# Attending the first batch in two halves of its queries, with MoE work beside the second half, and V loaded by a casting transfer

## The chip, the cores and the metric

The kernel runs on one core of one Trainium2 chip. The metric is device microseconds (us) of one execution, as a median over runs. Engines: PE is the matmul engine (PEld its weight loads), DVE the vector engine, ACT the scalar engine, POOL (Pool) GpSimd, SP the engine that issues most transfers. Ratios below are the mean time of one kernel's fast runs over that of the kernel before in the same rounds on the same chip, so they are not quite the ratio of the medians that stand beside them. The brackets behind a ratio are its 95% interval.

## The reference

```python
# q, k, v: [8 batches, 12 heads, 448, 64]; w_in: [768, 2048]; w_out: [2048, 768]
q_n, k_n = rmsnorm(q, g_q), rmsnorm(k, g_k)          # over the last axis
scores = q_n @ k_n.T / 8 ; scores -= max(scores)      # per query
attn = exp(scores) / sum(exp(scores))
x = (attn @ v), heads side by side                    # [3584, 768]
h = x @ w_in ; out = maximum(0.01 * h, h) @ w_out     # float32
```

The last line is called MoE in the kernel. It is two dense matrix products.

## The kernel before

The attention is cut into 24 units: a batch times three groups of four heads. Each unit is prepared (squares on ACT, their sums on DVE, the reciprocal root `rinv` on ACT, the normalised `n` on DVE), transposed to `qkT`, and then attended (scores `sT` on PE, exps `et` on ACT, the product with V on PE). The exps take a bound `eb` in place of the maximum: probe matmuls on PE, maxima `pm` and a diagonal `dg` on DVE, a matmul `pb` on PE, and `cm` and `eb` on DVE. Units 0 and 1 are transposed on PE (`prep_tr`), all later ones by a transpose transfer (`prep_trd`).

```python
def prep_v(u):                      # V arrives as float32, Pool casts it
    nc.gpsimd.tensor_copy(buf(u, "vt")..., hj(raw[u][2])...)
def prep_trd(u):                    # one transfer transposes q and k of a unit
    nc.sync.dma_start_transpose(out=buf(u, "qkT")..., in_=buf(u, "n16")...)
def qk_exp(u, i0, n):               # 8 score blocks and 8 exps a unit, 2 per quarter d
    ...
def moe1(b, ft):                    # 6 matmuls of 448 columns, then the leaky relu on ACT
    ...
for u in range(NU):
    for d in range(NJ):             # NJ = 4 quarters
        qk_exp(u, 2 * d, 2)
        ...                         # cut: unit 0 has its own order
        if d == 0:
            load(u + 3); pv(u - 1); prep_v(u + 2); prep_qg(u + 2, ...); prep_sq(u + 2)
            if u < 5: load_w_out(4 * (u - 1), 4)
        if d == 1 and u % NQ == 0:
            push_moe(u // NQ - 1)   # MoE of a batch, queued when its three units are done
        if d == 2: prep_probe(u + 1); prep_rinv(u + 2); prep_norm(u + 2, ...); prep_trd(u + 2)
        if d == 3: prep_shift(u + 1)
        fill(u, d)                  # takes MoE pieces from the queue
```

In these traces an instruction that waits holds the work that stands behind it on its engine.

Of the kernel before, what the change touches and what calls it, by code (L numbers as in the profile page):

```python
# [8 lines left out]
FP32 = mybir.dt.float32  # L9
FP16 = mybir.dt.float16  # L10
AF = mybir.ActivationFunctionType
# [7 lines left out]
def kernel(  # L19
# [24 lines left out]
    cst = ctx.enter_context(tc.tile_pool(name="cst", bufs=1))  # L44
    raws = ctx.enter_context(tc.tile_pool(name="raws", bufs=2))
    prep_p = ctx.enter_context(tc.tile_pool(name="prep", bufs=2))
# [41 lines left out]
    def load(u, parts=1):  # L88
        b, g = divmod(u, NQ)
        tiles = []  # L90
        for name in ("rq", "rk", "rv"):
            tiles.append(raws.tile([SP, QH, NJ, D], FP32, tag=name, name=name))
        n = QH // parts
        todo = [(i, p) for p in range(parts) for i in range(2)] + [(2, p) for p in range(parts)]
        for i, p in todo:
            src = (q, k, v)[i][b, QH * g + n * p:QH * g + n * p + n]
            nc.sync.dma_start(tiles[i][:, n * p:n * p + n], src.rearrange("h (p j) d -> p h j d", j=NJ))
        raw[u] = tiles
        st[u] = {}

    HJ = QH * NJ
# [3 lines left out]
    def hj(t):  # L105
        return t.rearrange("p h j d -> p (h j) d")

    SHAPES = dict(
        sq=([SP, 2, HJ, D], FP32, 1), ssq=([SP, 2, HJ], FP32, 2), uu=([SP, 2, HJ], FP32, 2),
        rinv=([SP, 2, HJ], FP32, 2), qg=([SP, HJ, D], FP32, 2), vt=([SP, QH, NJ, 2, D // 2], FP16, 4),  # L110
        n16=([SP, 2, 2, NJ, 2, D], FP16, 2), qkT=([128, 2, 2, NJ, SP], FP16, 3))
# [11 lines left out]
    def prep_qg(u, eng, c=ALL):  # L123
        n = c[1] - c[0]
        eng.tensor_tensor(buf(u, "qg")[:, c[0]:c[1]], hj(raw[u][0])[:, c[0]:c[1]],  # L125
                          ggb[:, None, :].broadcast_to([SP, n, D]), op=ALU.mult)

    def prep_v(u):
        nc.gpsimd.tensor_copy(buf(u, "vt").rearrange("p h j t d -> p (h j) t d"),  # L129
                              hj(raw[u][2]).rearrange("p j (d t) -> p j t d", t=2))  # L130

# [18 lines left out]

    def prep_tr(u, r):
        tp = aux([128, 2, NJ, SP], FP16, "tp")
        for ti in range(2):
            for j in range(NJ):
                nc.tensor.transpose(tp[:, ti, j, :],  # L155
                                    buf(u, "n16")[:, ti, r, j].rearrange("p a d -> p (a d)"),
                                    ident16[:SP, :])
        nc.vector.tensor_copy(buf(u, "qkT")[:, :, r], tp)

# [39 lines left out]
    def qk_exp(u, i0, n):  # L199
        s = st[u]  # L200
        if i0 == 0:
            s["et"] = epool.tile([SP, NJ, QH, S], FP16, tag="et", name="et")
        sTs = []
        for i in range(i0, i0 + n):
            r, jk = divmod(i, NJ)
            sT = psum.tile([SP, 2, 512], FP32, tag="sT", bufs=2, name="sT")
            for a in range(2):
                qT, kT = pair_qk(u, r, a)
                nc.tensor.matmul(sT[:, a, 0:S], kT[:, ts(jk, SP)], qT,  # L209
                                 start=True, stop=True)  # L210
            sTs.append(sT)
        for i, sT in zip(range(i0, i0 + n), sTs):
            r, jk = divmod(i, NJ)
            nc.scalar.activation(s["et"][:, jk, 2 * r:2 * r + 2, :], sT[:, :, 0:S], AF.Exp,  # L214
                                 bias=s["eb", r], scale=1.0)

    xts = {}

    def pv(u):
        s = st[u]  # L220
        b, g = divmod(u, NQ)
        if g == 0:
            xts[b] = xpool.tile([128, NQ, 2, S], FP16, tag="xt", name="xt")
        xt = xts[b]
        banks = []
        for w in (2, 0, 1):
            bank = aux([128, 512], FP32, "pv")
            for jk in range(NJ):
                for i in range(QH):
                    lhsT = ones16 if w == 2 else s["vt"][:, i, jk, w, :]  # L230
                    nc.tensor.matmul(bank[32 * i:32 * i + 32, 0:S], lhsT, s["et"][:, jk, i, :],  # L231
                                     start=(jk == 0), stop=(jk == NJ - 1))
            banks.append(bank)
            if w == 2:
                lz = zpool.tile([128, S], FP32, tag="lz", name="lz")
                nc.scalar.activation(lz, bank[:, 0:S], AF.Ln)
                rz = zpool.tile([128, S], FP32, tag="rz", name="rz")
                nc.scalar.activation(rz, lz, AF.Exp, bias=0.0, scale=-1.0)  # L238
            else:
                nc.vector.tensor_tensor(xt[:, g, w, :], bank[:, 0:S], rz, op=ALU.mult)  # L240

    def moe1(b, ft):
        xt = xts[b]
        hps = aux([128, 512], FP32, "hps")
        for kt in range(KT):
            nc.tensor.matmul(hps[:, 0:S], win16[:, kt // 2, kt % 2, ts(ft, 128)],  # L246
                             xt[:, kt // 2, kt % 2], start=(kt == 0), stop=(kt == KT - 1))
        nc.scalar.activation(gt[:, ft, ds(S * (b % 2), S)], hps[:, 0:S], AF.Prelu,  # L248
                             bias=0.0, scale=1.0, alpha=0.01)
# [25 lines left out]

    def push_moe(b):
        for ft in range(FT):
            queue.append((1.13, lambda b=b, ft=ft: moe1(b, ft)))
        for t in (range(3) if b % 2 == 0 else range(3, 7)):
            for half in range(2):  # L280
                queue.append((2.62, lambda b=b, t=t, half=half: moe2(b // 2, t, half)))
# [4 lines left out]
    def fill(u, d):  # L286
# [3 lines left out]
        while True:  # L290
# [5 lines left out]
            left += WD[dd]  # L296
        debt[0] += total * WD[d] / left
        while queue and debt[0] >= queue[0][0] * 0.5:
# [4 lines left out]
    with tc.manual_schedule():  # L303
        nc.scalar.dma_start(grow[:, 0], g_q[None, :])
        nc.scalar.dma_start(grow[:, 1], g_k[None, :])
        load(0, parts=2)
        load(1)
        nc.scalar.preload_act_table_set("natural_log_exp_and_others")
        nc.vector.tensor_tensor(grow[:, 0], grow[:, 0], grow[:, 1], op=ALU.mult)
# [5 lines left out]
        prep_qg(0, nc.vector, HALF[0])  # L315
        prep_ssq(0, HALF[0])
        prep_rinv(0, HALF[0])
        prep_norm(0, 0)
        prep_tr(0, 0)
        prep_sq(0, HALF[1])  # L320
        prep_probe(0, (0,))
        prep_v(0)
        prep_shift(0, (0,))
        prep_qg(0, nc.vector, HALF[1])
        prep_ssq(0, HALF[1])

        for u in range(NU):
            for d in range(NJ):
                qk_exp(u, 2 * d, 2)
                if u == 0:  # L330
                    if d == 0:
                        prep_rinv(0, HALF[1])
                        prep_norm(0, 1)
                        prep_tr(0, 1)
                        prep_probe(0, (1,))
                        prep_sq(1)
                        prep_v(1)
                        prep_qg(1, nc.vector)
                        prep_ssq(1)
                        load(2)  # L340
                        load_w_in(0, 512)
                        load_w_in(512, 512)
                        load_w_in(1024, 1024)
                        load(3)
                    if d == 1:
                        prep_shift(0, (1,))
                        prep_rinv(1)
                        prep_norm(1, 0)
                        prep_tr(1, 0)
                        prep_norm(1, 1)  # L350
                        prep_tr(1, 1)
                    if d == 2:
                        prep_probe(1)
                        prep_sq(2)
                        prep_v(2)
                        prep_qg(2, nc.vector)
                        prep_ssq(2)
                    if d == 3:
                        prep_shift(1)
                        prep_rinv(2)  # L360
                        prep_norm(2, 0)
                        prep_norm(2, 1)
                        prep_trd(2)
                    continue
                if d == 0:
                    if u + 3 < NU:
                        load(u + 3)
                    pv(u - 1)
                    if u + 2 < NU:
                        prep_v(u + 2)  # L370
                        prep_qg(u + 2, nc.vector if u == 1 else nc.gpsimd)
                        prep_sq(u + 2)
                    if u < 5:
                        load_w_out(4 * (u - 1), 4)
                if d == 1 and u % NQ == 0:
                    push_moe(u // NQ - 1)
                if u + 1 < NU:
# [13 lines left out]
        pv(NU - 1)  # L391
        push_moe(B - 1)
        while queue:
# [31 lines left out]
```

## Time and profile before

| kernel before | value |
|---|---|
| time, median of 4 runs | 471.83 us (471.44 to 472.27) |
| span of the profiled run | 470.1 us |
| first MoE matmul | 66.84 us |
| PE busy | 433.3 us, 92% of the span |
| ACT busy | 322.2 us, 69% |

The prediction below shows the overview, the stretches, the chain of waits and the timeline. Exps on ACT per stretch: stretch, its length, ACT time in exps (their number), granted clock, DMA share, GB/s.

```profile
20.00:40.00 20.00, 6.57 (x8) 1.00 1.14 242
40.00:60.00 20.00, 12.38 (x14) 0.66 1.16 243
60.00:80.00 20.00, 9.43 (x11) 0.83 0.96 175
```

The second view has the chain of waits (start, length, what) within 37 to 45 us, that is while the one transpose transfer of the chain, of unit 2, was under way:

```profile
37.64 7.11 DMA qkT<-n
```

### The profile page before, as it was taken

What the parts mean: (1) busy time and instruction counts of PE and PEld (TensorE: products, weight loads), DVE (VectorE), ACT (ScalarE), POOL (GpSimd) and SP (SyncE); (2) the same over time, 40 slices, a digit from 0 to 9 for tenths busy, and PEclk for the clock granted to TensorE, in tenths of its full rate; (3) what the DMA queues carried; (4) which work ended last, traced back from release to release, by engine and by line L of the source; (5) the groups of instructions that cost most, each with busy time, mean ns of one, the idle gap of its engine ahead of it and who ended that gap; (6) DMA issues with size and microseconds to landing.
All of it is one profiled execution on the core that took longest, in us unless ns stands there. A gap on an engine that the chain in (4) does not pass through costs nothing.

```text
span 470.1 us, 8104 instructions
## 1 busy us (share of the span) xinstructions
PE 433.3 (92%) x3355; PEld 218.6 (47%) x3355; DVE 273.4 (58%) x416; ACT 322.2 (69%) x469; POOL 88.0 (19%) x63
## 2 busy tenths in 40 slices
PE   2255799999999999999999999999999999999995
PEld 1122334455445544455455544454455544555563
DVE  4877656767756957666666766685665761211021
ACT  3558888976896588777877589867877588644400
POOL 1611333212312303320320210220320200000000
PEclk9998669999999999999999999999999999999999
DMA  8899998784485494376457466359438412021022
GB/s 208 172 240 235 250 224 136 169 191 89 135 158 120 107 225 93 72 184 144 112 126 173 95 182 143 66 140 210 79 95 193 106 35 40 0 68 35 0 68 67
DMA packets 82665, 60.95 MB, mean 130 GB/s; under 512 B 42436, under 2 KB 78276, under 8 KB 82628
## 3 DMA queue, kind: packets, MB, share of 16 engines
q1 hardware_dynamic: 78064, 54.14, 49.8%
q0 software_dynamic: 4560, 6.29, 7.9%
q8 instruction: 26, 0.43, 0.4%
q14 instruction: 11, 0.09, 0.1%
q10 hardware_dynamic: 4, 0.00, 0.0%
HBM read 45.61 MB, written 11.01 MB: 120 GB/s over the span
## 4 chain that ended last, share of the span: by engine, by line
PE 80%; DVE 9%; ACT 8%; DMA 2%; issue 1%; ACTq 0%; DVEq 0%
PE op L259 30%; PE hps L246 27%; PE pv L231 11%; PE sT L209 9%; DVE n L145 5%; ACT et L214 5%; DMA qkT<-n 2%; ACT sq L121 1%; PE probe L178 1%; DVE pm L181 1%; PE pb L191 1%; DVE dg L185 1%; PE tp L155 1%; DVE ssq L134 1%; ACT gt L248 1%
## 5 line engine op out<-in xcount | busy, mean ns | idle before, releaser
L214 ACT ACTIVATE et<-sT,eb 112x896 f16<-112x896 f32 x192 | 182.4, 1005 | 82.6 <-PE sT L209 67.9
L246 PE MATMUL hps<-xt,win 128*128 128x448 f16 x768 | 153.2, 353 | 0.0
L259 PE MATMUL op<-wout,gt 128*128 128x384 f16 x896 | 152.7, 326 | 0.0
L259 PEld LDWEIGHTS <-gt 128*128 128x128 f16 x896 | 85.5, 98 | 61.4 <-issue 7.5
L246 PEld LDWEIGHTS <-win 128*128 128x128 f16 x768 | 72.1, 98 | 72.0 <-issue 10.2
L248 ACT ACTIVATE gt<-hps 128x448 f16<-128x448 f32 x128 | 66.4, 542 | 27.5 <-PE hps L246 27.3
L129 POOL CAST vt<-rv 112x1024 f16<-112x1024 f32 x24 | 27.5, 1144 | 279.3 <-DMA rv<-in_v_dram 244.1
L209 PE MATMUL sT<-qkT 64*112 64x448 f16 x384 | 62.2, 395 | 7.8 <-ACT et L214 7.8
L262 DVE COPY ost<-op 128x384 f32<-128x384 f32 x56 | 31.0, 554 | 64.8 <-PE op L259 64.7
L240 DVE TENSOR_TENSOR xt<-pv,rz 128x448 f16<-128x448 f32 x48 | 27.9, 620 | 69.1 <-ACT rz L238 67.5
L145 DVE TENSOR_TENSOR n<-qg,rinv 112x512 f16<-112x512 f32 x48 | 56.3, 1173 | 8.3 <-ACT rinv L140 8.1
L134 DVE TENSOR_REDUCE ssq<-sq 112x16 f32<-112x1024 f32 (+1 forms) x50 | 56.3, 1167 | 0.0
L125 POOL TENSOR_TENSOR qg<-rq,ggb 112x1024 f32<-112x1024 f32 x20 | 51.2, 2559 | 0.0
L145 DVE TENSOR_TENSOR n<-rk,rinv 112x512 f16<-112x512 f32 x48 | 50.8, 1058 | 0.0
L181 DVE TENSOR_REDUCE pm<-probe 112x1 f32<-112x448 f32 (+1 forms) x50 | 28.0, 601 | 38.1 <-PE probe L178 37.3
L231 PE MATMUL pv<-et,vt 112*32 112x448 f16 x768 | 45.1, 381 | 0.0
L209 PEld LDWEIGHTS <-qkT 64*112 64x112 f16 x384 | 20.0, 131 | 44.9 <-issue 44.6
L231 PEld LDWEIGHTS <-vt 112*32 112x32 f16 x768 | 22.1, 104 | 18.8 <-issue 5.3
L121 ACT ACTIVATE sq<-rq 112x1024 f32<-112x1024 f32 (+1 forms) x25 | 25.2, 1007 | 1.0 <-DMA rq<-in_q_dram 1.0
L121 ACT ACTIVATE sq<-rk 112x1024 f32<-112x1024 f32 (+1 forms) x25 | 25.2, 1008 | 0.1
L231 PE MATMUL pv<-et,ones 112*32 112x448 f16 x384 | 24.8, 382 | 0.2 <-DVE cm L193 0.2
L155 PE MATMUL tp<-ident,n 112*128 112x112 f16 x32 | 4.4, 293 | 13.1 <-DVE n L145 12.9
(34 smaller groups left out, 126.5 us busy)
## 6 DMA issues: line engine op xcount, KB each, us to landing
rq<-in_q_dram SPq DMA_DIRECT2D x23, 448.0 KB, 5.6
rk<-in_k_dram SPq DMA_DIRECT2D x23, 448.0 KB, 6.6
rv<-in_v_dram SPq DMA_DIRECT2D x23, 448.0 KB, 7.3
wout<-in_moe_w_out_dram POOLq DMA_DIRECT2D x4, 768.0 KB, 9.5
out_dram<-ost SPq DMA_DIRECT2D x8, 336.0 KB, 2.8
out_dram<-ost SPq DMA_DIRECT2D x8, 288.0 KB, 3.5
out_dram<-ost SPq DMA_DIRECT2D x8, 240.0 KB, 4.6
win<-in_moe_w_in_dram POOLq DMA_DIRECT2D x6, 256.0 KB, 9.3
```

Of the source, the lines that this page charges most:

```text
L121: nc.scalar.activation(buf(u, "sq")[:, ti, c[0]:c[1]], hj(raw[u][ti])[:, c[0]:c[1]], AF.Square)
L125: eng.tensor_tensor(buf(u, "qg")[:, c[0]:c[1]], hj(raw[u][0])[:, c[0]:c[1]], ggb[:, None, :].broadcast_to([SP, n, D]), op=ALU.mult)
L134: nc.vector.tensor_reduce(buf(u, "ssq")[:, ti, c[0]:c[1]], buf(u, "sq")[:, ti, c[0]:c[1]], axis=AXL.X, op=ALU.add)
L145: nc.vector.tensor_tensor(buf(u, "n16")[:, ti, r].rearrange("p j a d -> p a j d"), src[:, 8 * r:8 * r + 8].rearrange("p (a j) d -> p a j d ...
L181: nc.vector.tensor_reduce(pm2[:, a:a + 1], probes[a][:, 0:224 * len(rs)], axis=AXL.X, op=ALU.max)
L209: nc.tensor.matmul(sT[:, a, 0:S], kT[:, ts(jk, SP)], qT, start=True, stop=True)
L214: nc.scalar.activation(s["et"][:, jk, 2 * r:2 * r + 2, :], sT[:, :, 0:S], AF.Exp, bias=s["eb", r], scale=1.0)
L231: nc.tensor.matmul(bank[32 * i:32 * i + 32, 0:S], lhsT, s["et"][:, jk, i, :], start=(jk == 0), stop=(jk == NJ - 1))
L246: nc.tensor.matmul(hps[:, 0:S], win16[:, kt // 2, kt % 2, ts(ft, 128)], xt[:, kt // 2, kt % 2], start=(kt == 0), stop=(kt == KT - 1))
L248: nc.scalar.activation(gt[:, ft, ds(S * (b % 2), S)], hps[:, 0:S], AF.Prelu, bias=0.0, scale=1.0, alpha=0.01)
L259: nc.tensor.matmul(op2[:, 0:HC], gt[:, ft, ts(t, 128)], wout16[:, ft, ds(HC * half, HC)], start=(ft == 0), stop=(ft == FT - 1))
L262: nc.vector.tensor_copy(ost[0][:, ds(HC * half, HC)], op2[:, 0:HC])
```

## The change

Its intent: PE waits in the first 67 us. If the three units of batch 0 are attended for the first half of their queries first, the first half of the batch's tokens has its x early, and the MoE of those tokens can fill PE beside the second half of the queries. Besides, V comes by a transfer that casts it on the way, which takes 24 casts from Pool. To make the start fit, unit 0 is prepared whole, the multiplies `qg` of the first units go from DVE to Pool, and unit 1 now goes through a transpose transfer. The core of the diff:

```diff
-        for name in ("rq", "rk", "rv"):
+        tiles = [... for name in ("rq", "rk")]
+    def load_v(u):
+        nc.gpsimd.dma_start(buf(u, "vt"), v[...])          # casts float32 to float16
-    def prep_v(u): ...
+    SH = S // 2
+    def qk_exp_half(u, half, r): ...                       # 4 exps of a unit's half, 224 queries
-    def pv(u):
+    def pv(u, half=None): ...                              # V weights now two elements apart
-    def moe1(b, ft):
+    def moe1(b, ft, c0, n): ...                            # n = 224 or 448 columns
+        early(0, 0)                # exps of unit 0, half 0; prepares unit 1 (prep_trd) and 2
+        prep_probe(1); prep_shift(1); load(3)
+        early(1, 0); pv(0, 0); early(0, 1); pv(1, 0)
+        prep_probe(2); prep_shift(2); load(4)
+        early(2, 0); ...; pv(0, 1); load_w_out(0, 4); early(1, 1)
+        ...; prep_trd(3); pv(2, 0); load(5); early(2, 1)
+        push_moe1(0, 0, SH)        # MoE, first half of the tokens
+        ...; pv(1, 1); load_w_out(4, 4)
+        spend(4.5)                 # some 4.5 us of MoE from the queue here
+        prep_rinv(4); prep_norm(4, 0); prep_norm(4, 1); prep_trd(4)
+        prep_probe(3); prep_shift(3)
+        spend(4.0)
-        for u in range(NU):
+        for u in range(NQ, NU):    # units from 3 on as before
...                                # cuts: start-up of unit 0, buffer counts
```

## The prediction

> **What bounds the kernel now.** I read the overview of the page first, then stretches of the span, then the chain that ended last, then the timeline of the first 100 us.
>
> The 40 slices (11.75 us each) show two regimes:
>
> ```profile
> PE   2255799999999999999999999999999999999995
> ...
> ACT  3558888976896588777877589867877588644400
> ```
>
> TensorE (PE) is nearly saturated from the seventh slice to the end; before that no engine is. The stretches give the same in microseconds (length, then busy time of PE, PEld, DVE, ACT, POOL, then clock, DMA share, GB/s):
>
> ```profile
> 0.00:67.00 67.00, 35.63 (x257) 15.71 (x258) 45.37 (x85) 43.36 (x60) 21.09 (x26) 0.85 1.05 217
> 67.00:120.00 53.00, 52.83 (x419) 26.45 (x419) 36.07 (x50) 42.14 (x62) 12.25 (x7) 1.00 0.76 162
> 120.00:200.00 80.00, 80.00 (x635) 40.05 (x639) 54.63 (x75) 62.28 (x94) 19.45 (x10) 1.00 0.55 127
> 200.00:300.00 100.00, 99.83 (x794) 50.61 (x787) 68.14 (x94) 77.76 (x115) 21.12 (x12) 1.00 0.59 138
> ```
>
> Busy time alone proves little for PE, but the chain of waits agrees: from the first MoE matmul (66.84) to the last copy it is matmul after matmul.
>
> ```profile
> 66.84 3.52 PE hps L246 x18
> ...
> 426.01 18.31 PE hps L246 x96
> 444.32 20.81 PE op L259 x128
> 465.15 0.56 DVE ost L262
> ```
>
> So: a start of 66.8 us, bound by a chain through ACT, DVE, PE and transfers; then 398.4 us (465.2 - 66.8) of dense PE work; then 5 us of last copy and store, span 470.1. The runs read about 1.7 us more than the span. Only two things can shorten the time: PE getting dense earlier, or less PE work. The change adds no PE speed, so the whole question is when PE gets dense and how much MoE work it has done by then.
>
> How the start hangs together shows in these lines of the timeline (start, length, instruction, idle time and releaser):
>
> ```profile
> 34.90 1.69 PE L231 MATMUL pv<-et,ones 112*32 112x448 f16 x16
> ...
> 45.45 1.16 DVE L181 TENSOR_REDUCE pm<-probe 112x1 f32<-112x448 f32 x2 [1.81 <-PE probe L178]
> ...
> 49.95 1.91 ACT L214 ACTIVATE et<-sT,eb 112x896 f16<-112x896 f32 x2 [2.21 <-DVE eb L195]
> ...
> 73.78 2.79 POOL L125 TENSOR_TENSOR qg<-rq,ggb 112x1024 f32<-112x1024 f32 x1
> ...
> 74.29 2.84 DVE L145 TENSOR_TENSOR n<-rk,rinv 112x512 f16<-112x512 f32 x1
> ...
> 77.99 0.94 PE L231 MATMUL pv<-et,ones 112*32 112x448 f16 x16
> ```
>
> Three readings. The same 16 matmuls take 1.69 us in the start and 0.94 us later. An exp waits for the bound eb, which comes 2.5 us after the probe matmuls even when DVE is free (two maxima 1.16, a small maximum, the diagonal 0.25, a matmul, a maximum, eb). And a normalisation takes 2.84 us beside a Pool multiply instead of its usual 0.68 us.
>
> **What the Trainium skill says.** "TensorE: Matmul & The Clock Gate", Part 1, says that the array runs at half clock until about 3.4 us of sustained work and falls back after an idle window as long. The 1.69 against 0.94 us agrees, though the clock row still reads full there at 35 us. "GPSIMD Engine Reference", 1. Specifications, says that GpSimd shares its SBUF interfaces with VectorE, with contention for DVE instructions with two SBUF inputs; the 2.84 us agree: the multiply ends at 76.57 and the normalisation 0.56 us later. "DMA: Bandwidth & Descriptors", SWDGE vs HWDGE vs iDMA, says a casting transfer must be issued from GpSimd; the weights already come that way (0.71 us of Pool each), so V by such a transfer costs Pool 0.7 us in place of a cast of 1.14 us.
>
> **The V part.** It removes 24 casts of 1.14 us (27 us of Pool) and 24 transfers from the SP queue, and adds 24 casting transfers. In the dense regime neither Pool nor DVE nor DMA (share 0.55 to 0.6) sets the end, so that is worth about 0. The weights of the PV matmuls become columns two elements apart; no trace here has such a load. The 48 matmuls of a unit take 2.38 us, one per 49.6 ns, near what 448 columns in four column groups need, and loads hide under that; I assume they still do. At the very start V of unit 0 now competes with q and k of unit 0, which the first squares wait for (before, V stood behind them in the queue): about 1 us lost.
>
> **The start, walked along the order of the built program** with durations from the trace (squares 1.0 each, four normalisations 2.4, two sums 2.3, exp pair 1.9, transpose transfer 5 to 7, the eb chain 2.5).
> - Unit 0 is prepared whole before any exp. Squares of its second half stand ahead of rinv of the first on ACT, and the sums of unit 1 (2.3 us) ahead of the maxima on DVE. First exp about 22.5 us; in the kernel before 12.3, but there only four exps were done by 21.
> - Four exps and the squares of unit 2 to 28.5. Unit 1 now goes through a transpose transfer; its normalisation stands behind a Pool multiply; the maxima of unit 1 also stand behind the normalisation of unit 2, at 33. Second batch of exps (unit 1) about 36, ACT idle some 6 us before it.
> - Eight exps (with a short PE wait) to 46; then bound of unit 2 after its PV and probe: about 50. Twelve more exps with three reciprocals (2 ACTIVATEs each, estimated 0.4 us at half width), squares of units 3 and 4, rinv: ACT is full to 68. The PV half of unit 1 ends on PE about 67, and there the first half of MoE begins.
>
> So MoE begins at about 67, just where it began before (66.8). All that the halves gained up to here is that PV of unit 2's second half (1.2 us) is not done yet: no gain.
>
> **From there**: 15 of the 16 half-width groups of the first MoE product stand before unit 3. Six matmuls of 195 ns (3.51/18) make 1.17 us at full width, so 0.6 warm and 1.2 cold at half width. Eight groups, some cold: 67 to 73.6. Then PE has probe and bound of unit 3 in its queue, ahead of the other seven. The bound needs the maxima on DVE; those stand behind the normalisation of unit 4; that waits for rinv of unit 4, which stands on ACT behind the eight Prelus. Sum: last Prelu 0.5, ln and exp 0.6, four normalisations 2.4, maxima 1.3, diagonal 0.3 = 5.1 us in which PE can do only the probe. PE resumes at about 79, cold again by its idle time; seven groups 4.2 to 6 us: 85. Scores of unit 3, the last PV half, the sixteenth group and waits for exps: 3 us. **MoE's second half starts at about 88**, where the kernel before stood at 66.8.
>
> Remaining work then: 398.4, less the 16 half groups already done (9.3), plus about 1 for matmuls of 224 columns that cannot run at twice the rate (estimate), plus 1 where units 3 and 4 have so little MoE left that ACT sets the pace (in one quarter of unit 4: 1.9 exps + 1.1 + 2.1 + Prelus against PE's 4.3) = 391. End of span 88 + 391 + 5 = 484, timed 486. I take 2 off because the array may stay warm through part of this: **484.0 us**, 2.6% slower.
>
> **The rivals.**
> 1. The intended gain: the halves pipeline, the start is shorter, and 9.3 us of MoE vanish into idle PE time. By the sum above, the second MoE half would have to begin before 470 - 391 - 5 = 74 merely to break even, and by 65 to be 2% faster. For: ACT has only 48 us of work before that point (43 before, plus 5 of Prelus). Against: the orders above leave ACT idle for some 14 us before the first exp, 6 before unit 1 and 3.5 before unit 2, and nothing in the order fills that. If the first exps come 5 us earlier and the wait at unit 3 is 3 us: 474.
> 2. The array clock falls less often than I assume and Pool's multiplies do not collide with normalisations: 478 to 480, counted as "same".
> 3. It is worse: the strided weight load no longer hides, or half-width matmuls are bound by the 98 ns weight load and more; 0.03 us on 192 matmuls is 6 us; or transposes queue behind 6.3 MB of weights read in the first 42 us: 490 or more.
>
> **Range and chances.** The late wait (5 us), the two ramps of the clock and the missing gain at 67 carry the sum; each start step is good to 1 or 2 us, together 5. Range 475 to 491. The 2% limit is 481.1, a little below the centre: slower 0.66; same 0.29; faster needs 462.2, which the ACT order forbids unless I misread it: 0.05.
>
> **What would show it.** Right: first exp near 22 us; ACT idle before exps of unit 1 and of unit 2; first half-width MoE matmul near 67; a PE gap of 4 to 5 us before the bound of unit 3 that ends on DVE's diagonal; second MoE half near 88; the stretches from 120 on with PE at 100% as before, and the last 40 us the same. Wrong: MoE beginning by 58, or no gap at the bound of unit 3, would mean a start shorter than walked. PV of a full unit over 2.5 us, or half-width matmuls over 115 ns apart, would mean that rival 3 pays. PE gaps after 150 us would mean that the bound moved to ACT or to V's arrival, which I do not expect.

## More of the kernel before

```profile
q0 software_dynamic: 269, 0.50, 33.3%
```

The software queue carries the casting loads of the weights. Their packets took a third of the DMA engines' time while the transpose of unit 2 ran. (The shares of the queues overlap and can add up to more than 100%.)

## The result and the profile after

| | before | after |
|---|---|---|
| time, median | 471.83 us (471.44 to 472.27, 4 runs) | 495.16 us (494.76 to 496.04, 4 runs) |
| ratio | | 1.050 [1.048, 1.052] |
| span | 470.1 us | 493.2 us |
| PE busy | 433.3 us | 435.5 us |
| first MoE matmul | 66.84 us | 73.71 us, half width |

The change costs 23.3 us. PE is busy for only 2.2 us more, so 21 of the 23 us are PE idling. The overview of the kernel after (40 slices, now of 12.3 us each, the digit is the busy share in tenths) has it in the first seven slices:

```profile
PE   1305676999999999999999999999999999999995
ACT  3533693798599676887787758976896578753400
```

Where the kernel before had PE at 5 and 5 in slices three and four and at 7, 9, 9 in five to seven, this one has 0, 5 and 6, 7, 6, and ACT has holes too. The stretches (length, busy time of PE, PEld, DVE, ACT, POOL, then clock, DMA share, GB/s) say when PE becomes dense:

```profile
80.00:93.50 13.50, 9.26 (x105) 7.29 (x105) 4.50 (x10) 4.95 (x12) 3.21 (x4) 0.75 0.92 178
93.50:120.00 26.50, 24.22 (x240) 15.89 (x242) 16.26 (x30) 23.97 (x44) 5.44 (x5) 1.00 0.62 112
120.00:140.00 20.00, 18.69 (x175) 9.70 (x164) 11.21 (x21) 13.88 (x19) 3.05 (x2) 1.00 0.71 168
140.00:200.00 60.00, 59.39 (x460) 30.17 (x460) 32.03 (x57) 45.84 (x69) 12.20 (x8) 1.00 0.60 120
200.00:300.00 100.00, 100.00 (x809) 50.43 (x807) 52.40 (x94) 76.27 (x110) 18.31 (x12) 1.00 0.56 122
```

From 140 us on PE is nearly as full as before (59.39 of 60 us, then 100 of 100), so the loss lies ahead of it. Between 93.5 and 120 us ACT is busy for 23.97 of 26.5 us: there PE loses 2.3 us with ACT nearly full. The timeline of the start (start, length, engine, line, instruction, in brackets the idle time before it and what ended it) shows the rest:

```profile
22.97 3.70 ACT L233 ACTIVATE et<-sT,eb 112x896 f16<-112x896 f32 x4 [1.92 <-PE sT L228]
...
40.38 0.62 PE L178 MATMUL probe<-qkT 64*112 64x224 f16 x4 [14.83 <-DMA qkT<-n]
43.57 3.70 ACT L233 ACTIVATE et<-sT,eb 112x896 f16<-112x896 f32 x4 [12.65 <-PE sT L228]
...
73.71 5.38 PE L265 MATMUL hps<-xt,win 128*128 128x224 f16 x48
...
84.24 0.34 PE L191 MATMUL pb<-dg,onesp 112*112 112x112 f16 x1 [4.82 <-DVE dg L185]
84.38 6.24 PE L265 MATMUL hps<-xt,win 128*128 128x224 f16 x42
...
93.53 2.95 PE L265 MATMUL hps<-xt,win 128*128 128x224 f16 x24
```

After four exps from 22.97 us on, ACT gets no exp until 43.57 us. PE stood 14.83 us at the probe of unit 1, for its transpose. The chain of waits gives that transfer its length:

```profile
28.07 12.26 DMA qkT<-n
```

Of the 23 transpose transfers of this kernel the median took 4.0 us, so this one took three times as long. The DMA queues within 28 to 41 us, the time of this transfer, show what it shared the engines with:

```profile
q0 software_dynamic: 1317, 1.82, 78.6%
```

The casting loads take 78.6% here, against 33.3% beside the transpose of the kernel before, and V is among them now. Last, the exps per stretch, as above:

```profile
20.00:40.00 20.00, 3.70 (x4) 1.00 1.18 192
40.00:60.00 20.00, 10.24 (x12) 0.95 1.05 200
60.00:80.00 20.00, 8.24 (x9) 0.63 0.31 71
80.00:100.00 20.00, 5.47 (x6) 0.83 0.85 155
```

There are 16 exps done by 60 us (26 before) and 25 by 80 us (37 before). The attention is 12 exps behind, which is one and a half units, when the MoE of the first half begins to pay.

### The profile page after: what moved, and what is told of

Read it like the earlier page. It is cut to its first block, busy times and chain, and to the rows that moved or that the text cites. A ratio compares the mean times of both kernels' runs of the same rounds, so it can differ in the third digit from the quotient of the medians.

```text
span 493.2 us, 8643 instructions
## 1 busy us (share of the span) xinstructions
PE 435.5 (88%) x3626; PEld 235.5 (48%) x3626; DVE 224.0 (45%) x408; ACT 326.8 (66%) x493; POOL 82.4 (17%) x67
## 4 chain that ended last, share of the span: by engine, by line
PE 80%; ACT 9%; DVE 5%; DMA 4%; issue 1%; SPq 0%; DVEq 0%; ACTq 0%
PE op L278 30%; PE hps L265 28%; PE pv L251 11%; PE sT L209 8%; ACT et L213 3%; DVE n L145 3%; DMA qkT<-n 2%; ACT et L233 2%; ACT sq L125 2%; DMA rk<-in_k_dram 2%; PE pb L191 1%; PE probe L178 1%; DVE pm L181 1%; PE sT L228 1%; DVE ssq L134 0%
## 5 line engine op out<-in xcount | busy, mean ns | idle before, releaser
L265 PE MATMUL hps<-xt,win 128*128 128x448 f16 (+1 forms) x864 | 157.1, 337 | 0.5 <-DVE cm L193 0.3
L129 POOL TENSOR_TENSOR qg<-rq,ggb 112x1024 f32<-112x1024 f32 (+1 forms) x24 | 55.6, 2315 | 301.8 <-DMA rq<-in_q_dram 276.6
L267 ACT ACTIVATE gt<-hps 128x448 f16<-128x448 f32 (+1 forms) x144 | 68.6, 503 | 36.7 <-PE hps L265 36.5
L259 DVE TENSOR_TENSOR xt<-pv,rz 128x448 f16<-128x448 f32 (+1 forms) x54 | 28.6, 568 | 95.1 <-ACT rz L257 94.7
L209 PE MATMUL sT<-qkT 64*112 64x448 f16 x336 | 50.0, 371 | 3.7 <-ACT et L213 3.6
L251 PE MATMUL pv<-et,vt 112*32 112x448 f16 (+1 forms) x864 | 44.9, 357 | 0.0
L181 DVE TENSOR_REDUCE pm<-probe 112x1 f32<-112x448 f32 x48 | 27.7, 619 | 37.6 <-PE probe L178 36.5
L145 DVE TENSOR_TENSOR n<-qg,rinv 112x512 f16<-112x512 f32 x48 | 33.2, 691 | 23.5 <-ACT rinv L140 14.4
L145 DVE TENSOR_TENSOR n<-rk,rinv 112x512 f16<-112x512 f32 x48 | 35.6, 742 | 0.0
L251 PE MATMUL pv<-et,ones 112*32 112x448 f16 (+1 forms) x432 | 25.0, 358 | 0.0
```

The lines of the kernel that those rows point to most:

```text
L129: eng.tensor_tensor(buf(u, "qg")[:, c[0]:c[1]], hj(raw[u][0])[:, c[0]:c[1]], ggb[:, None, :].broadcast_to([SP, n, D]), op=ALU.mult)
L145: nc.vector.tensor_tensor(buf(u, "n16")[:, ti, r].rearrange("p j a d -> p a j d"), src[:, 8 * r:8 * r + 8].rearrange("p (a j) d -> p a j d ...
L181: nc.vector.tensor_reduce(pm2[:, a:a + 1], probes[a][:, 0:224 * len(rs)], axis=AXL.X, op=ALU.max)
L209: nc.tensor.matmul(sT[:, a, 0:S], kT[:, ts(jk, SP)], qT, start=True, stop=True)
L251: nc.tensor.matmul(bank[32 * i:32 * i + 32, 0:n], lhsT, et[:, jk, i, 0:n], start=(jk == 0), stop=(jk == NJ - 1))
L265: nc.tensor.matmul(hps[:, 0:n], win16[:, kt // 2, kt % 2, ts(ft, 128)], xt[:, kt // 2, kt % 2, ds(c0, n)], start=(kt == 0), stop=(kt == KT ...
```

## The experiments

Two theories stood against each other. **Collisions**: the halves are sound, and the loss is the slow transposes and the wait at the bound of unit 3. **Halves**: the halves lose by themselves, since unit 3 begins only when the second halves are done, and the collisions come on top. All runs gave correct results. A third question was whether V had a part.

### V alone

The kernel before, with V by the casting transfer and the weights of PV two elements apart, and nothing else.

```diff
-        nc.gpsimd.tensor_copy(buf(u, "vt")..., hj(raw[u][2])...)
+        nc.gpsimd.dma_start(buf(u, "vt"), v[b, QH * g:QH * g + QH].rearrange("h (p j) d -> p h j d", j=NJ))
-        lhsT = ... s["vt"][:, i, jk, w, :]
+        lhsT = ... s["vt"][:, i, jk].rearrange("p (d t) -> p t d", t=2)[:, w]
```

> The kernel before with one part of the change alone: V by casting transfers, where the casts stood, and the PV weights at every second column. Theory (V part is worth about nothing, the loss is all in the new order of the start): within 1.5 us of 471.9, PV of a full unit still 2.4 us, TensorE dense from 120 us on. Rival (V by such transfers, or the strided weight loads, cost the time): 476 or more, PV over 2.5 us.

Measured: 473.48 us (472.75 to 474.21, 6 runs) against 471.87, ratio 1.003 [1.001, 1.005]. V is worth 1.6 us of the 23.3 and the strided weights nothing that shows.

### Unit 1 transposed on PE

```diff
-                    prep_trd(1)
+                if (u, half, r) == (0, 0, 1):
+                    prep_tr(1, 0, nc.vector.tensor_copy)
+                    prep_tr(1, 1, nc.vector.tensor_copy)
```

> The changed kernel with one thing undone: unit 1 is transposed by 16 matmuls and two DVE copies, as before the change, instead of by a transfer. Theory (the 12.3 us transpose transfer of unit 1 holds the second batch of exps back): exps of unit 1 begin at about 36 instead of 43.6 us, everything behind them moves by the same 7 us, timed about 488. Rival (the transfer is hidden, because the transfer of unit 2, which landed at 41.9, or another chain would end just as late): under 2 us gained, 493 or more.

Measured: 488.30 us (486.76 to 488.96) against 471.93, ratio 1.034 [1.031, 1.037]. The exps of unit 1 begin at 37.5 us and the second MoE half at 87.4 us. The transfer was worth 6.9 us (495.16 - 488.30).

### The weight loads moved instead

The same wait can be taken away from the other side: the transfer stays, and `w_in` is loaded later.

```diff
-        load_w_in(0, 512); load_w_in(512, 512); load_w_in(1024, 1024)
         prep_rinv(1)
 ...
         prep_qg(3, nc.gpsimd)
+        load_w_in(0, 512); load_w_in(512, 512); load_w_in(1024, 1024)
```

> The changed kernel with the nine loads of the first weights issued behind the Pool multiply of unit 3 (about 47 us) instead of at 16 to 24 us. Theory (the transpose transfer is slow because these loads hold the DMA engines): the transposes of units 1 and 2 land 5 to 6 us after issue, exps of unit 1 begin at about 36 us, and the time falls by about 7 to 488, less what the first MoE matmul then waits for its weights (they need some 20 us, so until 67 to 70, where MoE would begin: 0 to 3 us lost). Rival (a transpose transfer at this place is slow by itself, two in a row): landing still 8 us and more, no gain.

Measured: 492.10 us (491.83 to 493.25), ratio 1.043 [1.040, 1.046]. It is short of the expectation (488, and 0 to 3 us more), and tells the most about the mechanism. The transposes of units 1 and 2 landed in some 4 us now, and the exps of unit 1 began at 35.2 us. But the chain of waits of this run shows that the wait went with the loads:

```profile
62.07 15.24 DMA qkT<-n
77.35 0.66 PE probe L178 x4
```

The transpose of unit 3 was issued beside the moved loads and took 15.2 us, with PE at the probe behind it. To be exact, the last `w_in` load landed at some 63.5 us; what lay beside the rest of this transpose were two `w_out` loads that had been pushed back behind `w_in` (the second landed 21.8 us after its issue, against 9.0 in the kernel after). Casting packets took 74.1% of the engines' time from 62 to 77 us.

### The bound of unit 3 first

```diff
         spend(4.5)
-        prep_rinv(4); prep_norm(4, 0); prep_norm(4, 1); prep_trd(4)
         prep_probe(3)
-        prep_shift(3)
         spend(4.0)
+        prep_shift(3)
+        prep_rinv(4); prep_norm(4, 0); prep_norm(4, 1); prep_trd(4)
```

> The changed kernel with the bound of unit 3 put ahead of the preparation of unit 4, and its last matmul behind the seven second groups of MoE. Theory (the 4.8 us gap of PE at 79.4 to 84.2 and the half clock behind it are lost time): no PE gap there, the seven groups take 4.2 instead of 6.2 us, second MoE half 5 to 7 us earlier, timed 488 to 490. Rival (ACT and the late preparation of unit 4 set the pace of units 3 and 4 anyway, so the gap only moves): under 2 us gained.

Measured: 491.42 us (491.02 to 493.30), ratio 1.042 [1.039, 1.045]: 3.7 us under the kernel after, and so less than the 5 to 7 us expected. Its timeline has no gap ahead of the bound:

```profile
81.71 4.20 PE L265 MATMUL hps<-xt,win 128*128 128x224 f16 x42
85.74 0.21 PE L191 MATMUL pb<-dg,onesp 112*112 112x112 f16 x1
```

The 42 matmuls take 4.20 us in place of 6.24: without the idle time the array does not fall to half rate. In the kernel after, the leaky relus behind these matmuls show that rate: the first come 1.12 us apart, the last 0.57. A part of the gain was lost ahead of them: in this run the first 48 matmuls of MoE begin at 75.00 us and take 6.44 us, against 73.71 and 5.38 in the kernel after.

### Both together

> The changed kernel with two repairs together: unit 1 transposed on TensorE, and the bound of unit 3 ahead of the preparation of unit 4. Theory (the two losses lie one behind the other): 495.2 - 6.9 - 3.7 = 484.5, that is still 12 to 13 us slower than the kernel before. Rival (they overlap, the first repair uncovers the wait of the second elsewhere): 487 or more. In both cases the MoE of the first half begins at about 67 to 68 us, no earlier than MoE began in the kernel before.

Measured: 485.27 us (483.73 to 486.26), ratio 1.028 [1.025, 1.031]. The parts add up nearly (6.9 + 3.7 expected, 9.9 found). Both named waits are gone and 13.4 us of the loss are left, so the theory of these two collisions alone is refuted.

### MoE work not beside the second half

```diff
-        push_moe1(0, 0, SH)
-        spend(4.5)
-        spend(4.0)
```
with the whole MoE of batch 0 at full width from unit 3 on.

> The changed kernel with the attention of batch 0 in halves, but its MoE at full width and only after unit 3 has begun, as in the kernel before. Theory (the MoE work put beside the second half delays unit 3 by more than it saves, because it stands in the way of the bound of unit 3): MoE begins at about 82 to 83 with 398 us of work behind it, timed 487 to 489, so faster than the changed kernel by 6 to 8 us. Rival (the MoE work beside is a gain of its 9.3 us, and the loss is all in the start): timed 503 or more.

Measured: 497.36 us (496.50 to 500.11), ratio 1.055 [1.051, 1.060]: neither expectation. The transpose of unit 4 took 13.45 us here, beside a `w_out` load, and PE idled for 3.49 us at the probe, until 93.58 us. The run was not a clean answer, so it was repeated on a kernel without the other waits.

### The same question, with the other waits taken away

`e8_clear` is the combination above with the last two `w_out` loads moved away from transposes; `e7_clear_no_moe` is the same without MoE beside the second half.

```diff
-                    if u < NQ + 2:
-                        load_w_out(8 + 4 * (u - NQ), 4)
+                if u == NQ and d == 1: load_w_out(8, 4)
+                if u == NQ + 1 and d == 2: load_w_out(12, 4)
```

> The changed kernel with three repairs: the two of e5_pe_tr1_bound3, and the last two loads of the second weights moved away from the transposes of units 4 and 5 (in e5_pe_tr1_bound3 the transpose of unit 5 took 9.6 us beside such a load and TensorE stood for it). Theory (transposes beside weight loads are the recurring wait): 5 to 7 us less than 485.3, so 478 to 481, still slower than the kernel before because MoE begins no earlier. Rival (units 3 to 5 are bound by ACT anyway): 484 or more.

> e8_clear without the MoE work beside the second half: batch 0 in halves, its MoE at full width once unit 3 has begun. It asks what that work is worth when no transpose and no bound stands in the way. Theory (it delays unit 3 by nearly what it saves): MoE begins at 74 to 76 with 398 us behind it, within 4 us of e8_clear either way. Rival (it is worth its 9.3 us of matmuls): slower than e8_clear by 7 to 10 us.

Measured: 484.44 us (480.84 to 485.60), ratio 1.025 [1.020, 1.029], and 484.11 us (484.01 to 484.49), ratio 1.025 [1.022, 1.029]. Moving the `w_out` loads gained about 1 us, within the spread of the runs, where 5 to 7 had been expected. The MoE work beside the second half, which the halves exist for, is worth nothing here, as the theory of the second run had it. (`e7_clear_no_moe` still waits for a transpose at two probes, 1.75 and 0.57 us; without these it would be faster, not slower.)

### Whole units with the other parts of the change

`c1_whole` keeps V, the loads and the start of the kernel after, but attends whole units. Units 1 and 2 are transposed on PE, and in units 1 and 2 the bound goes ahead of the next preparation.

```diff
-        early(0, 0) ... early(2, 1)        # and all between
-        for u in range(NQ, NU):
+        for u in range(NU):
             for d in range(NJ):
                 qk_exp(u, 2 * d, 2)
+                if u == 0: ...              # prepares 1 and 2, prep_tr(1, ...)
+                if u == 1 and d == 1: prep_tr(2, 0, ...); prep_tr(2, 1, ...)
-                    if d == 2:
+                    if d == (3 if u < 3 else 2):
                         prep_rinv(u + 2) ...
```

> The changed kernel with the halves undone: its loads, its V, its preparation of unit 0 as a whole and its Pool multiplies stay, but batch 0 is attended in whole units, MoE of batch 0 comes after unit 3 has begun, and units 1 and 2 are transposed on TensorE. Theory (the halves are the loss: they bring MoE no earlier and split every bound, PV and wait in two): eight exps of unit 0 from 23 us on, unit 1 from 32 to 33, unit 2 from 43, MoE begins at 57 to 62, timed 462 to 467, faster than both kernels. Rival (the new preparation at the start is what costs): MoE begins at 67 or later, 472 or more.

Measured: 468.56 us (467.04 to 470.09), ratio 0.993 [0.989, 0.996], the first version under the kernel before. But it differs from the halves in more than one thing: the units, the transposes of units 1 and 2, the order of the bounds, and the places of the `w_out` loads, which are those of the kernel before. Its chain of waits still holds one transfer, of unit 4, with PE at the probe until 67.1 us:

```profile
59.29 7.81 DMA qkT<-n
```

### Three attempts to improve single parts

`c2_whole_clear` moves the second and third `w_out` load of `c1_whole` one unit ahead and puts the preparation of unit 4 back into its old quarter. `b12_before_tr2_bound` and `b3_before_tr2` give the kernel before a unit 2 transposed on PE, with the bound first in two units or in one (that edit, of the same line as in `c1_whole`, is cut below).

```diff
+                    if u == 1: load_w_out(0, 4); load_w_out(4, 4)          # c2
+                    if u in (2, 4): load_w_out(4 * (u // 2 + 1), 4)        # c2
-                        prep_trd(2)                                        # b12, b3
+                        prep_tr(2, 0) ... prep_tr(2, 1)                    # b12, b3
```

> c1_whole with the two things repaired that its trace shows: the normalisation and transpose of unit 4 go back to the third quarter of unit 2, and no load of the second weights is issued beside it (the 7.8 us transpose from 59.3 on held TensorE to 67.5). Theory: TensorE is dense from 59.5 us on, 4 to 6 us less than 468.6, so 463 to 465, faster than the kernel before by 1.5 to 1.9%. Rival (the next wait takes its place): 467 or more.

> The kernel before with two small edits that follow from what the others showed: unit 2 transposed on TensorE instead of by a transfer that took 7.1 us, and in units 1 and 2 the bound of the next unit ahead of the normalisation of the one after it. Theory (transfers beside weight loads and normalisations ahead of bounds are the waits of the start in this kernel too): MoE begins 3 to 5 us earlier than 66.8, timed 467 to 469. Rival (another chain ends at the same time): 471 or more.

> The kernel before with unit 2 transposed on TensorE, and only in unit 1 the bound of the next unit ahead of the normalisation (in b12_before_tr2_bound unit 2 had that too, which sent the transpose of unit 4 off late; its runs fell into 473 to 475 and 480 to 483). Theory: no slow group of runs, 467 to 470. Rival (TensorE transposes and their DVE copies cost the start as much as the transfer did): 472 or more.

All three missed. `c2_whole_clear`: 471.34 us (470.86 to 472.75), ratio 0.999 [0.996, 1.002]; the transpose of unit 3 took 10.56 us beside the advanced loads, so once more the wait moved with the loads. `b12_before_tr2_bound` falls into two groups, 473.0 to 474.8 (3 runs) and 480.7 to 483.2 us (5 runs), with a median of 480.94 over all; its fast runs have the ratio 1.003 [0.999, 1.007], and its profile is of the slow group, where the transpose of unit 4 took 8.38 us. Why it has two groups is open. `b3_before_tr2`: 475.31 us (473.52 to 476.13), ratio 1.006 [1.002, 1.010]; its chain has a transpose of unit 3 of 6.53 us, and I did not settle where the rest goes.

### The halves against whole units, with equal transposes

Two pairs were run to separate the halves from the transposes. First the combination of both fixes with whole units and unit 2 by the transfer, as there:

```diff
 # against c1_whole
-                    prep_tr(2, 0, nc.vector.tensor_copy)
-                    prep_tr(2, 1, nc.vector.tensor_copy)
+                    prep_trd(2)
```

> e5_pe_tr1_bound3 with whole units in place of the halves and nothing else moved on purpose: unit 1 on PE, unit 2 by the transpose transfer, bound of unit 3 ahead of the preparation of unit 4, MoE from unit 3 on. So it isolates the halves, which c1_whole did not (it also put unit 2 on PE). Theory, that the halves themselves cost the rest: near c1_whole, 468 to 474, thus 11 us or more under e5's 485.3. Rival, that what c1_whole won came from unit 2 on PE: 480 to 485, no better than e5.

Measured: 479.41 us (478.15 to 484.40), ratio 1.017 [1.011, 1.024], between the two expectations. The chain of waits says why:

```profile
37.36 16.55 DMA qkT<-n
53.91 0.04 issue
53.95 0.67 PE probe L178 x3
```

Whole units wait for the whole transposition of unit 2. In the halves nothing waits: there a transpose issued at 34.35 us is first needed at 47.3 us, since the second half of unit 0 lies between. But one more thing moved. The first two `w_out` loads, which in `e5_pe_tr1_bound3` are issued at 43.39 and 47.22 us, are issued at 29.78 and 40.24 us here, beside the transpose (casting packets take 86.2% of the engines' time from 37 to 54 us). How long the transpose took in the halves their trace does not say. So this pair compares halves without a wait against whole units with one transfer of 16.6 us in the chain, and whole units still win by 5.9 us. Unit 2 on PE is worth 10.8 us of `c1_whole` (479.41 - 468.56).

Then a pair with units 1 to 4 on PE in both, so that no transpose transfer is needed while the weights arrive:

```diff
 # f2_whole_pe4, against c1_whole
+                if u in (2, 3) and d == 1:
+                    prep_tr(u + 1, 0, nc.vector.tensor_copy)
+                    prep_tr(u + 1, 1, nc.vector.tensor_copy)
-                        prep_trd(u + 2)
+                        if u + 2 > 4:
+                            prep_trd(u + 2)
 # e9_halves_pe4, against e5_pe_tr1_bound3
-                    prep_trd(2)   # and prep_trd(3), prep_trd(4)
+                    prep_tr(2, 0, ...); prep_tr(2, 1, ...)   # the same for 3 and 4
```

> c1_whole with units 3 and 4 transposed on PE as well, ahead of their probes, so that none of the first five units waits for a transpose transfer beside the weight loads. Theory, that the 7.8 us transpose of unit 4 held PE in c1_whole: 4 to 6 us less, 463 to 465, and no PE gap over 3 us between 60 and 90. Rival, that ACT sets the pace there or the wait moves to unit 5: 467 to 470.

> e5_pe_tr1_bound3 with units 2, 3 and 4 transposed on PE as well: the halves with every early transpose off the transfers, thus the counterpart of f2_whole_pe4 (466.9), from which it differs by the halves (and the MoE work beside them). If the halves cost time by themselves, because unit 3 and its exps begin only when the second halves are done: 479 to 484, some 12 to 17 above f2_whole_pe4. If the halves only lost through waits for transposes beside the loads, and whole units gain the same from transposes on PE: at most 472.

> f2_whole_pe4 again, on the chip of e9_halves_pe4, so that the two share the runs of the kernel before and the best version is timed twice: 465 to 468, ratio 0.985 to 0.992.

Measured: `f2_whole_pe4` 466.94 us (464.63 to 468.05), ratio 0.988 [0.984, 0.992], and again, on the chip of `e9_halves_pe4`, 466.00 us (465.67 to 466.80), ratio 0.986 [0.982, 0.990]. `e9_halves_pe4` 483.20 us (481.92 to 485.31), ratio 1.024 [1.018, 1.029]. The expectation for the first was 463 to 465, so it is a bit short of that; the second fell as expected, and so did `e9_halves_pe4`. The pair gives **17.2 us for the halves together with the order of work that goes with them** (483.20 - 466.00). What lies behind it shows in the stretches, first of the whole units (`f2_again`), then of the halves (columns as in the stretches above):

```profile
60.00:80.00 20.00, 20.00 (x169) 9.44 (x162) 11.83 (x20) 17.17 (x27) 4.12 (x4) 0.95 0.64 127
80.00:100.00 20.00, 20.00 (x161) 10.33 (x159) 9.95 (x19) 15.40 (x23) 4.59 (x4) 1.00 0.47 99
```

```profile
60.00:80.00 20.00, 19.00 (x267) 15.96 (x259) 10.70 (x21) 14.87 (x32) 4.14 (x3) 0.80 0.39 75
80.00:100.00 20.00, 17.64 (x196) 12.95 (x196) 12.97 (x23) 19.83 (x39) 5.49 (x4) 1.00 0.62 121
```

With whole units PE is full from 60 us on. With halves it is not, and between 80 and 100 us ACT is busy for 19.83 of 20 us: from these stretches it has become the bound. Before that, ACT had too little to do. Its timeline in the halves says why, here for the exps of unit 0 and of unit 1:

```profile
23.09 3.70 ACT L233 ACTIVATE et<-sT,eb 112x896 f16<-112x896 f32 x4 [2.09 <-PE sT L228]
...
37.77 1.91 ACT L233 ACTIVATE et<-sT,eb 112x896 f16<-112x896 f32 x2 [5.84 <-PE sT L228]
```

A half of unit 0 has four exps, 3.7 us, and then ACT waits for the bound of unit 1. With whole units there are eight exps to cover the same preparation. But that is not all of this wait. The probe of unit 1 is done at 29.54 us, and its maxima begin 4.9 us later, behind the sums and the normalisation of unit 2 on DVE:

```profile
28.98 2.33 DVE L134 TENSOR_REDUCE ssq<-sq 112x16 f32<-112x1024 f32 x2
...
33.84 0.68 DVE L145 TENSOR_TENSOR n<-rk,rinv 112x512 f16<-112x512 f32 x1
34.45 1.14 DVE L181 TENSOR_REDUCE pm<-probe 112x1 f32<-112x448 f32 x2
```

In `f2_again` the maxima begin at once (30.61, the probe done at 30.58) and the sums of unit 2 come behind the bound. So most of the 5.84 us that ACT waits here may come from the order on DVE and not from the halves, and the 17.2 us need not be the price of the halves alone. No run tried the halves with the other order. Exps done by 40, 60 and 80 us are 6, 20 and 27 with halves, and 12, 27 and 36 with whole units (the same view of exps per stretch as above).

For the two profiled runs the sum closes nearly (they lie 15.3 us apart, the medians 17.2). The last copy starts at 475.56 and 460.30 us, 15.3 us apart, and PE is full in both from 140 us on, so the halves are 15.3 us of PE work behind at 140. Between 62.9 and 140 us PE spent 47.5 us on MoE matmuls with halves (31.01 + 16.45) and 58.3 with whole units (38.48 + 19.86): 10.9 us of the 15.3. By 140 us the halves also are six exps behind (60 against 66), which is three quarters of a unit; at 2.38 us of PV and 8 x 0.26 us of scores a unit that is 3.3 us more. About 1 us is not booked.

## Why the prediction was wrong

The direction was right and the size was not: 484.0 predicted, 475 to 491 as the range, 495.2 measured. The sum had three terms that failed, and they make the whole difference of 11.2 us.

- **"Transpose transfer 5 to 7" in the walk of the start: this is the step that failed.** It measured 12.3 us. The exps of unit 1 came at 43.6 and not at 36, ACT was idle for 12.65 us and not "some 6", and MoE began at 73.7 and not at 67. Of these 6.7 us, 5.5 arrive at the second MoE half (93.5 for the predicted 88). The run with unit 1 on PE gains 6.9 us, and the run with the loads moved shows the cause: the transposes that no longer lay beside the loads took some 4 us, the one that now lay beside the pushed-back loads took 15.2. I took the duration from the kernel before (7.11), where the casting loads took 33.3% of the engines' time beside the transpose and not 78.6%. The effect stood in my third rival ("transposes queue behind 6.3 MB of weights", 490 or more), without a sum for it; it belonged in the walk.
- **"Remaining work 391"**: it was 394.7 (488.26 - 93.53). The term of 1 us for an ACT that sets the pace in units 3 and 4 was too small. PE lost 2.3 us between 93.5 and 120 us with ACT at 90%, and 1.3 us between 120 and 140 us.
- **"I take 2 off because the array may stay warm"**: it did not; the 42 matmuls after the gap took 6.24 us, just above my own 4.2 to 6.

What held: the first exp (22.97 for 22.5), the gap ahead of the bound of unit 3 (4.82 us idle on PE, ended by DVE's diagonal, for 5.1), the half rate after it, ACT's wait ahead of unit 2 (3.69 us for 3.5), the V part (1.6 us, for "about 0" and "about 1 us lost" at the start), PV of a full unit at an unchanged 2.38 us, half-width matmuls at 0.10 us (24 in 2.47 us), and a steady state as before. So of rival 3 only the branch of the queueing transposes came true. One sum was wrong: rival 1's 474 does not follow from its own terms, since first exps 5 us earlier and a wait of 3 us for 5.1 take 7.1 us off 484.0, to about 477. One thing was right in its outcome and thin in its reason. "No gain up to here" compared the times at which MoE begins, but the exps say more: by 80 us the attention is 12 exps behind, and no MoE work beside the second half pays for it, since `e7_clear_no_moe` and `e8_clear` are equal. In the order of the experiments the loss of 23.3 us over the kernel before, and the 6.2 us that the best version gains on it, part like this (medians of different chips, whose kernels before agree within 0.6 us):

| step | time, us | worth |
|---|---|---|
| kernel after | 495.16 | |
| unit 1 transposed on PE | 488.30 | 6.9 |
| bound of unit 3 ahead of unit 4's preparation | 485.27 | 3.0 |
| units 2 to 4 transposed on PE | 483.20 | 2.1, within the spread of the runs |
| whole units in place of the halves, with their order of work | 466.00 | 17.2 |
| kernel before, on that chip | 472.25 | |

So the halves in this order cost more (17.2 us) than the collisions (12.0, the first three steps). They may have a merit that the last pair hides: they need the transpose of unit 2 only 12.9 us after its issue (47.26 - 34.35). Whether they would have hidden one that takes 16.6 us, as it did with whole units, was not run. What stays open: the 17.2 us belong to the halves in this order. The maxima of unit 1 stand behind the normalisation of unit 2 on DVE, and 15 half groups of MoE (each six matmuls of 224 columns and a leaky relu) stand ahead of the first scores of unit 3. Another order might lose less. That ACT is the bound in units 3 to 5 is read from the stretches and not isolated by a run of its own. Nor does any run separate casting loads from plain ones: the transpose of 7.11 us in the kernel before lay beside both.

## What to carry to other kernels

Read a start by how much work of its slowest chain is done by a given time, here exps on ACT, and not only by when the bound engine gets its first work; cutting a unit in two also halves what covers the preparation of the next one, so the order of that preparation matters more. A transpose transfer has no fixed duration: beside bulk casting loads it took two to four times its usual 4 us, and moving the loads only moved the wait, until the transposes of the loading phase were done on PE. The parts of a change are worth testing apart: the new start, V by a casting transfer, PE transposes and an earlier bound with whole units make a version at 466 to 467 us, 1.2 and 1.4% under the kernel before in two sets of rounds, which is less than 2%. The part that gave the change its name costs 17 us on top, in the one order that was tried. Which part of that version gains is not isolated: V alone cost 1.6 us, and unit 2 on PE with an earlier bound gained nothing on the kernel before.

## What the Trainium skill lacked or had wrong

- "DMA: Bandwidth & Descriptors", Queues, rings and completion order, says that each DMA engine takes turns between its queues, a packet at a time. The slow transposes fit that, but no run here looks at single packets. What the page has no number for is the cost: one transpose of a unit took 4.0 us as a median and 12.3, 13.5, 15.2 and 16.6 us beside casting loads.
- "DMA: Bandwidth & Descriptors", Rules for kernel authors, says of correctness that "A transpose next to ordinary DMAs needs nothing". All runs were correct, so it agrees; but a reader who takes it for the time as well loses 7 to 11 us here.
- "TensorE: Matmul & The Clock Gate", Part 1, agrees with the half rate after idle time: 42 half-width matmuls took 6.24 us after a gap of 4.82 us and 4.20 us without one. The page cautions that the clock events can't be fully trusted. Here the granted clock reads 1.00 in the 20 to 40 us stretch of both kernels, where the kernel before spends 1.69 us on matmuls that take 0.94 us later.
- "DMA: Bandwidth & Descriptors", Alternative transpose paths, lists the transpose on TensorE as "useful when data already on-chip", and the runs agree that it works. What no page has a number for is what it is worth while bulk loads are under way: here 10.8 us for one unit in the whole-unit version (479.41 to 468.56), 6.9 for one in the halves (495.16 to 488.30), and nothing for one in the kernel before, there with an earlier bound.
